# New instruction orders, a row of w4 in column halves, and roots on ScalarE in a two-layer spectral mixer kernel

## The chip, the cores and the metric

The kernel runs on one core of a Trainium2 chip. A core has TensorE (matrix products, called PE in the profile, its weight loads PEld), VectorE (DVE), ScalarE (ACT), GpSimd (POOL) and SyncE (SP), each with its own queue of instructions, worked off in order; an instruction waits at the head of its queue until what it reads has been written. DMA transfers are issued from the queues of SP, ScalarE and POOL. The metric is the device time of one execution in microseconds (us); the time before is the median of five runs.

## What is computed

Two layers, each a spectral filter followed by an MLP with token shifts, on x of 2048 tokens by 512 channels:

```python
def _A_ref(x, w_r, w_i):
    X = rfft2(x.astype(float32), axes=(-2, -1))
    X = X * (w_r + 1j * w_i)
    return irfft2(X, s=(S, D), axes=(-2, -1)).astype(bfloat16)

def _B_ref(x, w1, w2, w3, w4):
    h = _gelu(_layernorm(x, axis=-1) @ w1)
    c = D // 4
    g0 = jnp.pad(h[:, :, 0*c:1*c], ((0, 0), (1, 0), (0, 0)))[:, :S, :]
    g1 = jnp.pad(h[:, :, 1*c:2*c], ((0, 0), (0, 1), (0, 0)))[:, 1:, :]
    ...
    hs = jnp.concatenate([g0, g1, g2, g3], axis=-1) @ w2
    x1 = x + hs
    h2 = _gelu(_layernorm(x1, axis=-1) @ w3) @ w4
    return x1 + h2

x = A_x
x = x + _A_ref(_layernorm(x, axis=-1), A_w_r, A_w_i)
x = x + _B_ref(_layernorm(x, axis=-1), B_w1, B_w2, B_w3, B_w4)
x = x + _A_ref(_layernorm(x, axis=-1), A_w_r, A_w_i)
x = x + _B_ref(_layernorm(x, axis=-1), B_w1, B_w2, B_w3, B_w4)
```

A layernorm divides by the square root of the variance plus 1e-5, without gain or shift. Both layers use the same weights.

## The kernel before

Token 16 p + q lies in partition p and row q, so x is held as `K.x`, 128 partitions by 16 rows by 512 channels. All matrix products are bfloat16 with float32 sums in eight PSUM banks.

The order of all work is written out by hand in three strings. `ORDER_0` (L764) is the first front, `ORDER_A` (L769) is layer 0 with the front of layer 1 at its end, and `ORDER_B` (L788) is layer 1. A word is a letter for the operation and a number for the row, unit or group; the letter after the number is the engine (V for VectorE, A for ScalarE), the number after a dot the first PSUM bank. Words are emitted in that order, and every engine takes its own in that order. `manual_schedule` leaves it so. A word of `FLEX` (m, G, n, o, t, x, Y) can go to either engine.

The stages of a layer, with their letters:

- **Front.** Statistics of each row (s, or B in a later layer: bn_stats on VectorE, L266; rows 1 and 5 of the first front as sums on ScalarE), aggregation (i, or j; L295), the inverse deviation (S: a Sqrt on ScalarE and the reciprocal J on VectorE in the first front; two POOL operations with a power of -0.5, L302 and L303, in `rstd4`). The DFT table T is scaled by it (Q, 256 columns a row) and multiplied with x (O, four matmuls of 256 columns a row; `over_p`, or `over_p_plain` for five pairs of rows). The result is copied into V (G).
- **Spectral stage.** For ten units of one or two blocks (`UNITS`): over channels (d, 4 matmuls of 256 columns a block, L484), copy TV (t); over rows (q, on 64 partitions, L508), copy X (x); the product with the weights W (p, VectorE, L527); back over rows (b, 8 matmuls of 128 columns, L538), copy into hT (m). X has two buffers, TV and Y share four.
- **Back transforms.** Over channels (D, 8 matmuls of 256 columns for two rows, L556), copy Y; over tokens (P, 4 matmuls of 256 columns a row, L568); the residual add with a sum (a, VectorE, L576).
- **First norm.** A square with a sum on ScalarE (s, L279); for a group of four rows, the moments and the inverse deviation on POOL (r: `from_sums`, `rstd_twice`, `shift`; the power is L313) and a ratio used later (c, L315 to L323); the normalized rows (n); their transposition by DMA from SP's queue (T, `turn`, L592).
- **Mixer.** w1 (v, L607), gelu (h, L614), w2 with the token shifts (u, L623), residual (f, L631), second norm (k, R, o), its transposition (U).
- **MLP.** w3 (w, 8 matmuls of 512 columns, L658), gelu (g, L665), w4 (W, 14 matmuls of 512 columns a row, L671), residual (A, L676). Layer 1 stores each row (y). Layer 0 goes on with the front of layer 1. In layer 0 the words L and N reorder W and negate a part of the table TR.

`ROWS` (L760) gives the order of rows in the MLP and the next front: index 14 is row 0 and 15 is row 1. `fill` (L250) issues matmuls on zeros: `WAKE` (44) of them at the start, 2 or 3 behind some fronts of the first stage, and those of X words in the orders (X4.4 is four, into bank 4). At the end of `ORDER_A` there are 16.

Weights W come by 16 DMAs on SP's queue (`load_W`) behind the eight loads of x; row 32 of W, for both planes, by two DMAs on POOL's queue (L172). They are doubled across partitions by four DMAs on POOL's queue, W<-W (L183). The MLP weights follow on SP's queue behind a small gate transfer (L201).

Words z load the gelu table of ScalarE ahead of need (`gelu_table`, L728).

Of the kernel before, what the change touches and what calls it, by code (L numbers as in the profile page):

```python
# [153 lines left out]
def load_all(K, A_x, A_w_r, A_w_i, B_w1, B_w2, B_w3, B_w4):  # L154
# [16 lines left out]
    for pl, v in enumerate(planes):  # L171
        nc.gpsimd.dma_start(K.W[2::4, pl, 0], v[:, 32])  # L172
# [38 lines left out]
    nc.vector.memset(K.eps[:], EPS)  # L211
    K.mhalf = K.const.tile([P, 4], FP32, name="mhalf")
# [42 lines left out]
class Stats:  # L255
# [8 lines left out]
    def bn(self, i, src):  # L264
        st = self.K.small.tile([P, 6], FP32, name="ln_st")
        self.K.nc.vector.bn_stats(st[:], src)  # L266
        self.st[i] = st[:]
# [26 lines left out]
    def aggr(self, i):  # L294
        self.K.nc.vector.bn_aggr(self.mv[:, i, :], self.st.pop(i))  # L295
# [9 lines left out]
    def rstd_twice(self):  # L305

        K = self.K
        e = K.nc.gpsimd
        self.ve2 = ve2 = K.small.tile([P, 4], FP32, name="ln_ve2")
        self.r = K.small.tile([P, 4], FP32, name="ln_r")  # L310
        e.tensor_scalar(ve2[:], self.mv[:, :, 1], 0.0, 1.0 + EPS, op0=ALU.max, op1=ALU.mult)
        e.tensor_scalar(ve2[:], ve2[:], EPS * EPS, None, op0=ALU.add)
        e.tensor_tensor(self.r[:], ve2[:], K.mhalf[:], op=ALU.pow)  # L313

    def ratio(self):  # L315
        K = self.K
        e = K.nc.gpsimd
        ve = K.small.tile([P, 4], FP32, name="ln_ve")
        self.c = K.small.tile([P, 4], FP32, name="ln_c")
        e.tensor_scalar(ve[:], self.mv[:, :, 1], 0.0, EPS, op0=ALU.max, op1=ALU.add)  # L320
        e.tensor_tensor(ve[:], ve[:], K.mhalf[:], op=ALU.pow)
        e.tensor_tensor(self.ve2[:], self.ve2[:], self.r[:], op=ALU.mult)
        e.tensor_tensor(self.c[:], self.ve2[:], ve[:], op=ALU.mult)  # L323
# [88 lines left out]
def first_front(K):  # L412
# [47 lines left out]
    K.load_mlp()  # L460


def layer(K, last):
# [118 lines left out]
    def rstd2(g):  # L582
        ln[g].from_sums()
        ln[g].rstd_twice()
        ln[g].shift()
# [80 lines left out]

    def w4(n):
        g, i = divmod(n, 4)
        ps["W", n] = o = banks(K, 1)[:, 0]
        for t in range(14):  # L670
            nc.tensor.matmul(o, lhsT=gT[g][:, t, i * P:(i + 1) * P], rhs=K.w4[:, t, :],  # L671
                             start=(t == 0), stop=(t == 13))

    def add_x2(n):
        q = ROWS[n]
        nc.vector.tensor_tensor(K.x[:, q, :], ps.pop(("W", n)), K.x[:, q, :], op=ALU.add)  # L676
# [4 lines left out]
    def stats4(n):  # L681
        k, i = divmod(n, 4) if n < 12 else (n, 0)
        if k not in lnA:
            lnA[k] = Stats(K, n=4 if n < 12 else 1)
        lnA[k].bn(i, K.x[:, ROWS[n], :])
# [5 lines left out]
    def rstd4(k):  # L691
        lnA[k].rstd()
# [5 lines left out]
    def front(k):  # L698
        qs = [ROWS[n] for n in PAIRS[k]]
        ps["O", k] = over_p_plain(K, qs) if k < PLAIN else over_p(K, qs, k == 15)  # L700

    def take_front(k, eng):
# [9 lines left out]
        else:  # L712
            take_V(K, qs, ps["O", k], eng, k == 15)
# [14 lines left out]
    def gelu_table(_):  # L728

        t = K.small.tile([P, 1], FP32, name="wake")  # L730
        nc.scalar.activation(t[:], K.eps[:], ACT.Gelu_apprx_tanh, bias=0.0, scale=1.0)

    next_V = {}
    table = {"z": gelu_table, "d": over_d, "t": take_d, "q": over_q, "x": take_q, "p": weigh, "b": back_q,
# [22 lines left out]
UNITS = {b: [b, b + 1] if 2 <= b < 14 else [b] for b in (0, 1, 2, 4, 6, 8, 10, 12, 14, 15)}  # L757
LATE = ((14, 15), (0, 14))
# [6 lines left out]
s0 s2 i2 s3 i3 i0 s1 f0 s4 S0 J0 i4 Q1V Q0V s5 Q3V s6 s7 i6 i7 Q2A s11 s10 O0 G0A f1 S1 J1 s8 O1 G1A Q6A s9 Q7A i10  # L765
i11 Q4A i9 i8 S2 s12 Q5A J2 Q10A O3 s13 G3A Q11V i13 i12 Q9V Q8V s14 S3 s15 i14 i15 O2 J3 Q12V G2A S4 J4 O5 G5A Q15A
Q13V Q14V O4 G4V O6 G6A O7 G7V O8 G8V G8A
"""
ORDER_A = """  # L769
d0.5 t0A d1.7 t1V N0 d2.2 t2A q1.4 x1A q0.6 x0V p0 d4.0 p1 t4A d10.6 t10V d6.4 t6V q2.2 q4.6 x2A p2 x4A p4 d12.0 t12A  # L770
q10.3 q6.5 b0.7 x6A m0V b1.2 m1V p6 d8.0 x10A b5.5 b3.6 m5V t8A d15.7 m3A b2.2 p10 q8.0 m2A N1 t15V q12.4 x8A x12A
b4.2 p8 p12 d14.6 t14A b10.1 b11.3 m11A b6.7 m6V q14.5 x14A p14 q15.3 b9.0 m10A x15A p15 b7.6 m7A m9V b12.5 m12A m4A
b13.1 m13V b8.3 m8A b14.4 m14A b15.5 m15A m15V D1.2 D0.4 D3.6 Y0A Y3A Y1V P2.1 a2 P3.4 P0.3 P1.0 s2 a3 s3 a0 s0 a1 s1
D2.1 D4.4 Y4A P6.0 P7.3 Y2V a6 s6 a7 s7 P4.6 a4 P5.1 P9.4 D5.2 a5 r0 n0V s4 n1V s5 T0 r1 n3V P8.5 n2V Y5A D6.6 Y6A
D7.0 a9 Y7A a8 P11.4 a11 s11 n6V c0 n7V P10.3 n4V P15.1 s9 P12.0 s8 P14.2 n5V a10 a15 T1 a12 P13.5 a13 s10 r2 n9V n11V
n8V v0.6 v1.4 h0 c1 a14 T3 h1 T2 v3.0 s15 v2.6 s13 h3 u0.4 n10V T5 h2 u1.2 s12 f1 s14 u2.1 f2 k1 r3 c3 f0 E0 u3.7 n14V
T4 n15V f3 v5.2 n12A h5 v4.1 h4 u4.6 n13V k3 f4 L14 u5.5 u7.3 c2 k2 k0 E1 R0 f7 L13 E7 u6.7 T7 f5 T6 v6.1 E2 k4 h6 o1V
o2V o0A v7.3 E3 h7 u13.2 f6 o3A u11.6 f11 k11 k7 L12 u10.7 u15.1 f15 U0 f13 E13 f10 k10 u8.5 f8 u12.3 f12 u14.6 k5 U1
k6 w3.1 f14 E14 g3 z0 k13 L3 w1.5 g1 w4.0 g4 w0.3 g0 w2.1 g2 u9.5 f9 E6 k14 E9 E5 w6.3 E10 g6 w5.0 R1 g5 k8 E4 o4V o5V
L15 U2 W2.5 A2 W1.2 L7 o7V W0.3 A0 B2 k9 R2 j2 A1 o6A o10V U3 B0 w8.0 w7.4 L9 w12.6 g12 g8 W3.2 E8 g7 L2 B1 o9A w10.0  # L780
g10 w9.3 g9 E11 j0 L1 A3 o8A k12 B3 j3 o11A w11.0 g11 j1 S0 k15 w13.6 R3 g13 W5.2 W4.0 A5 U4 W6.3 U5 w17.6 A4 Q3 A6 B6
# [53 lines left out]
```

## Time and profile before

| what | us |
|---|---|
| median of five runs (349.51 to 351.24) | 350.13 |
| the profiled execution, its own time | 350.12 |
| its span, first to last instruction | 348.3 |
| first front, from the first real matmul to layer 0's first d | 8.25 to 19.28 |
| spectral stage of layer 0, to its first D | 19.28 to 39.40 |
| back transforms, norm, w1 of layer 0, to its first w2 | 39.40 to 61.34 |
| rest of layer 0, to the end of its last w4 row | 61.34 to 180.54 |
| layer boundary, to layer 1's first d | 180.54 to 185.45 |
| spectral stage of layer 1 | 185.45 to 205.30 |
| back transforms, norm, w1 of layer 1 | 205.30 to 226.93 |
| rest of layer 1, to its last residual add | 226.93 to 345.23 |

Matmuls overlap: one with 512 columns lasts 0.379 us in the profile, but the next starts 0.216 later. So the busy share of TensorE hides what it waits for, and the starts have to be compared. The granted TensorE clock is 0.999 over the span. The lines of the other tables are counted by instruction, with their mean duration: a square of a row 0.62 on ScalarE, a copy of 1024 columns 1.02 on ScalarE and 1.22 on VectorE, a statistic of a row 0.683 on VectorE.

### The profile page before, as it was taken

How to read it: one execution, taken by the hardware profiler on the slowest of the kernel's cores; microseconds unless marked ns; L12 is line 12 of the kernel's file. 1: busy time of each engine (PE TensorE's matmuls, PEld its weight loads, DVE VectorE, ACT ScalarE, POOL GpSimd, SP SyncE). 2: the span in 40 equal slices, each digit the busy share in tenths (PEclk: the TensorE clock that was granted, in tenths of full speed). 3: DMA queues.
4: the chain of work that ended last, by engine and by line, in shares of the span. 5: the costliest groups of instructions: out<-in, count | busy, mean ns of one | idle time of the engine just before them, and what ended most of it. 6: DMA issues, size and time to landing. Idle time of an engine off the chain costs nothing.

```text
span 348.3 us, 5561 instructions
## 1 busy us (share of the span) xinstructions
PE 338.8 (97%) x2120; PEld 188.5 (54%) x2120; DVE 185.8 (53%) x435; ACT 194.2 (56%) x337; POOL 73.5 (21%) x178
## 2 busy tenths in 40 slices
PE   8899999999999999999999999999999999999995
PEld 6668885444444444444558888544444444444442
DVE  5989796587439041285895979746514300302011
ACT  5969799766614714323417979984373373232230
POOL 4660056632020300002020005572004000100000
PEclk9999999999999999999999999999999999999999
DMA  7987935441020300210000001643002400300202
GB/s 236 308 307 249 374 91 101 82 69 19 7 55 1 60 2 0 55 37 1 0 2 0 2 2 29 122 94 62 1 2 49 102 0 2 75 0 2 90 15 90
DMA packets 44938, 24.35 MB, mean 70 GB/s; under 512 B 34768, under 2 KB 41904, under 8 KB 44912
## 3 DMA queue, kind: packets, MB, share of 16 engines
q1 hardware_dynamic: 43600, 19.97, 22.8%
q0 software_dynamic: 1168, 3.97, 3.4%
q8 instruction: 16, 0.26, 0.3%
q14 instruction: 10, 0.08, 0.1%
q10 hardware_dynamic: 144, 0.07, 0.1%
HBM read 11.41 MB, written 2.10 MB: 39 GB/s over the span
## 4 chain that ended last, share of the span: by engine, by line
PE 78%; DMA 9%; DVE 6%; ACT 3%; issue 1%; SPq 1%; DVEq 0%
PE ps L671 28%; PE ps L658 28%; PE ps L623 8%; PE ps L607 7%; DMA W<-in_A_w_i_dram 4%; PE ps L556 3%; DVE PB L527 2%; DMA xT<-xn 2%; DMA x_state<-in_A_x_dram 2%; PE ps L568 2%; DMA W<-W 1%; ACT hT L151 1%; ACT X L151 1%; DVE x_state L576 1%; DVE hT L149 1%
## 5 line engine op out<-in xcount | busy, mean ns | idle before, releaser
L665 ACT ACTIVATE gT<-ps 128x1024 bf16<-128x1024 f32 x56 | 56.0, 1022 | 87.3 <-PE ps L658 87.2
L658 PE MATMUL ps<-xT,w 128*128 128x512 bf16 x448 | 99.1, 379 | 0.0
L671 PE MATMUL ps<-w,gT 128*128 128x512 bf16 x448 | 99.1, 379 | 0.0
L676 DVE TENSOR_TENSOR x_state<-ps,x_state 128x512 bf16<-128x512 f32 x32 | 21.8, 688 | 99.2 <-PE ps L671 99.2
L658 PEld LDWEIGHTS <-w 128*128 128x128 bf16 x448 | 43.8, 98 | 52.6
L671 PEld LDWEIGHTS <-gT 128*128 128x128 bf16 x448 | 43.7, 98 | 52.4
L631 DVE SCALAR_TENSOR_TENSOR xn<-xn,ln_c,ps 128x512 bf16<-128x512 bf16 x32 | 23.2, 744 | 33.2 <-PE ps L623 26.0
L623 PE MATMUL ps<-w,hT 128*128 128x512 bf16 x128 | 29.1, 379 | 0.0
L607 PE MATMUL ps<-xT,w 128*128 128x512 bf16 x128 | 28.8, 379 | 0.3 <-DMA xT<-xn 0.3
L279 ACT ACTIVATE junk<-xn 128x512 bf16<-128x512 bf16 x32 | 19.9, 622 | 12.7 <-DVE xn L631 12.7
L285 POOL TENSOR_SCALAR ln_mv<-ln_s 128x4 f32<-128x4 f32 x16 | 4.6, 289 | 83.9 <-DVE x_state L576 49.6
L266 DVE BATCH_NORM_STATS2 ln_st<-x_state 128x6 f32<-128x512 bf16 x30 | 20.1, 683 | 3.4 <-DMA x_state<-in_A_x_dram 2.9
L576 DVE SCALAR_TENSOR_TENSOR x_state<-ps,x_state 128x512 bf16<-128x512 f32 x32 | 20.4, 685 | 1.9 <-PE ps L568 1.8
L614 ACT ACTIVATE hT<-ps 128x512 bf16<-128x512 f32 x32 | 18.0, 593 | 5.9 <-PE ps L607 5.5
L607 PEld LDWEIGHTS <-w 128*128 128x128 bf16 x128 | 12.3, 98 | 15.6 <-DMA xT<-xn 0.6
L623 PEld LDWEIGHTS <-hT 128*128 128x128 bf16 x128 | 12.5, 98 | 15.1 <-ACT hT L614 0.2
L279 ACT ACTIVATE xn<-x_state 128x512 bf16<-128x512 bf16 x32 | 19.8, 621 | 0.4
L527 DVE TENSOR_TENSOR PB<-X,W 128x2048 bf16<-128x2048 bf16 (+1 forms) x20 | 19.4, 1010 | 0.4 <-ACT X L151 0.2
L302 POOL TENSOR_SCALAR ln_ve<-ln_mv 128x4 f32<-128x4 f32 (+1 forms) x15 | 4.1, 274 | 70.4 <-DVE ln_mv L295 69.7
L484 PE MATMUL ps<-FA,V 128*128 128x256 bf16 x128 | 15.8, 273 | 0.7 <-ACT V L151 0.5
L538 PE MATMUL ps<-TR,PB 128*128 128x128 bf16 x256 | 16.3, 219 | 0.1
L568 PE MATMUL ps<-Y,Tinv 128*128 128x256 bf16 x128 | 15.6, 272 | 0.7 <-ACT Y L151 0.7
(83 smaller groups left out, 398.5 us busy)
## 6 DMA issues: line engine op xcount, KB each, us to landing
w<-in_B_w_dram SPq DMA_DIRECT2D x2, 1792.0 KB, 12.4
W<-W POOLq DMA_DIRECT2D x4, 514.0 KB, 5.0
x_state<-in_A_x_dram SPq DMA_DIRECT2D x8, 256.0 KB, 6.0
out_dram<-x_state SPq DMA_DIRECT2D x16, 128.0 KB, 1.9
TR<-tab_TR POOLq DMA_DIRECT2D x2, 512.0 KB, 6.5
w<-in_B_w_dram SPq DMA_DIRECT2D x2, 512.0 KB, 5.7
W<-in_A_w_r_dram SPq DMA_DIRECT2D x7, 128.5 KB, 7.8
W<-in_A_w_i_dram SPq DMA_DIRECT2D x7, 128.5 KB, 7.6
```

The source lines that it names most:

```text
L266: self.K.nc.vector.bn_stats(st[:], src)
L279: K.nc.scalar.activation(out, src, ACT.Square, bias=0.0, scale=D ** -0.5, accum_out=self.s[:, i, 1:2])
L527: nc.vector.tensor_tensor(t, X.pop(u)[:, 0:2 * n].unsqueeze(1).to_broadcast([P, 2, 2 * n, 256]), K.W[:, :, 2 * u:2 * u + 2 * n, 1:257], op ...
L568: nc.tensor.matmul(o[:, h * 256:(h + 1) * 256], lhsT=K.Tinv[:, c], rhs=rhs[:, ::-1] if h else rhs, start=(e == 0), stop=(e == 1))
L576: nc.vector.scalar_tensor_tensor(K.x[:, q, :], ps.pop(("P", q)), 1.0, K.x[:, q, :], op0=ALU.mult, op1=ALU.add, accum_out=ln[g].s[:, i, 0:1])
L607: nc.tensor.matmul(o[:, i], lhsT=K.w1[:, t, j * P:(j + 1) * P], rhs=xT[g][:, :, t, :], start=(t == 0), stop=(t == 3))
L623: nc.tensor.matmul(o, lhsT=K.hT[:, j, st:st + P], rhs=K.w2[:, j, :], start=(j == 0), stop=(j == 3))
L631: nc.vector.scalar_tensor_tensor(xn[:, q, :], xn[:, q, :], ln[q // 4].c[:, q % 4:q % 4 + 1], ps.pop(("u", n)), op0=ALU.mult, op1=ALU.add, ...
L658: nc.tensor.matmul(o[:, i], lhsT=K.w3[:, c, t * P:(t + 1) * P], rhs=xT3[g][:, :, c, :], start=(c == 0), stop=(c == 3))
L665: nc.scalar.activation(gT[g][:, 2 * j:2 * j + 2, :], ps.pop(("w", k)), ACT.Gelu_apprx_tanh, bias=0.0, scale=1.0)
L671: nc.tensor.matmul(o, lhsT=gT[g][:, t, i * P:(i + 1) * P], rhs=K.w4[:, t, :], start=(t == 0), stop=(t == 13))
L676: nc.vector.tensor_tensor(K.x[:, q, :], ps.pop(("W", n)), K.x[:, q, :], op=ALU.add)
```

## The change

Six things change.

1. The two DMAs that load row 32 of W are issued from ScalarE's queue.
2. Behind the loads of the MLP weights, SP's queue gets one transposing DMA of the tile of zeros into a spare tile of the xT buffers.
3. In layer 0 the row with index 14 goes through w4 in two halves of 256 columns (words W14 and W24, A14 and A24, B14 and B24); its statistics are two partial ones, aggregated together.
4. For groups 0 and 1 of the first norm of each layer the deviation is a Sqrt on ScalarE (e) and a reciprocal on VectorE (i), in place of a power on POOL; the ratio takes the deviation.
5. For the rows with indices 12 to 15 in the front of layer 1 the same is done with `std` and `invert` (S and J).
6. The front of index 14 is split over two banks and copied by both engines, as that of index 15 was, and all three orders are new, with new engines for some copies and other numbers of dummy matmuls (7 at the end of `ORDER_A`, 4 ahead of its first d).

```diff
-        nc.gpsimd.dma_start(K.W[2::4, pl, 0], v[:, 32])
+        nc.scalar.dma_start(K.W[2::4, pl, 0], v[:, 32])
...
+    K.eps2 = K.const.tile([P, 1], FP32, name="eps2")
+    nc.gpsimd.memset(K.eps2[:], EPS * EPS)
...
-    def bn(self, i, src):
-        st = self.K.small.tile([P, 6], FP32, name="ln_st")
-        self.K.nc.vector.bn_stats(st[:], src)
-        self.st[i] = st[:]
+    def bn(self, i, src, part=(0, 1)):
+        k, n = part
+        if i not in self.st:
+            self.st[i] = self.K.small.tile([P, n, 6], FP32, name="ln_st", padded_shape=[P, 2, 6])[:]
+        self.K.nc.vector.bn_stats(self.st[i][:, int(k)], src)
...
+    def rstd_twice(self, root=False):
...
+        self.root = root
         e.tensor_scalar(ve2[:], self.mv[:, :, 1], 0.0, 1.0 + EPS, op0=ALU.max, op1=ALU.mult)
+        if root:
+            return
         e.tensor_scalar(ve2[:], ve2[:], EPS * EPS, None, op0=ALU.add)
         e.tensor_tensor(self.r[:], ve2[:], K.mhalf[:], op=ALU.pow)
+
+    def std_twice(self):
+        K = self.K
+        self.sd = K.small.tile([P, 4], FP32, name="ln_sd", bufs=4)
+        K.nc.scalar.activation(self.sd[:], self.ve2[:], ACT.Sqrt, bias=K.eps2[:], scale=1.0)
+
+    def invert_twice(self):
+        self.K.nc.vector.reciprocal(self.r[:], self.sd[:])
+        self.shift()
...
         e.tensor_tensor(ve[:], ve[:], K.mhalf[:], op=ALU.pow)
+        if self.root:
+            e.tensor_tensor(self.c[:], self.sd[:], ve[:], op=ALU.mult)
+            return
...
+    spare = K.grp.tile([P, 4, 4, P], BF16, name="xT", bufs=4)
+    K.nc.sync.dma_start_transpose(spare[:, 0, 0:1], K.zeros[:])
...
-        ln[g].rstd_twice()
-        ln[g].shift()
+        ln[g].rstd_twice(g in ROOT)
+        if g not in ROOT:
+            ln[g].shift()
...
+    def columns(n):
+
+        if last or n % 10 != 4 or n < 14:
+            return n, slice(0, D)
+        return 14, slice(0, D // 2) if n == 14 else slice(D // 2, D)
...
-        ps["W", n] = o = banks(K, 1)[:, 0]
+        r, d = columns(n)
+        g, i = divmod(r, 4)
+        ps["W", n] = o = banks(K, 1)[:, 0, 0:d.stop - d.start]
         for t in range(14):
-            nc.tensor.matmul(o, lhsT=gT[g][:, t, i * P:(i + 1) * P], rhs=K.w4[:, t, :],
+            nc.tensor.matmul(o, lhsT=gT[g][:, t, i * P:(i + 1) * P], rhs=K.w4[:, t, d],
                              start=(t == 0), stop=(t == 13))
...
     def rstd4(k):
-        lnA[k].rstd()
+        if k < 12:
+            lnA[k].rstd()
+        else:
+            lnA[k].std()
+
+    def invert4(k):
+        lnA[k].invert()
...
-        ps["O", k] = over_p_plain(K, qs) if k < PLAIN else over_p(K, qs, k == 15)
+        ps["O", k] = over_p_plain(K, qs) if k < PLAIN else over_p(K, qs, k >= 14)
...
+ROOT = (0, 1)
```

`add_x2` and `stats4` take the same columns, and `take_front` splits its copy for k >= 14. `gelu_table` becomes `act_table`, whose word z0 still loads the gelu table. Of the orders, the parts that the prediction walks through:

```diff
-s0 s2 i2 s3 i3 i0 s1 f0 s4 S0 J0 i4 Q1V Q0V s5 Q3V s6 s7 i6 i7 Q2A s11 s10 O0 G0A f1 S1 J1 s8 O1 G1A Q6A s9 Q7A i10
-i11 Q4A i9 i8 S2 s12 Q5A J2 Q10A O3 s13 G3A Q11V i13 i12 Q9V Q8V s14 S3 s15 i14 i15 O2 J3 Q12V G2A S4 J4 O5 G5A Q15A
-Q13V Q14V O4 G4V O6 G6A O7 G7V O8 G8V G8A
+s0 s2 s3 i0 i2 i3 s1 f0 S0 s4 J0 Q2V Q3V O1 i4 s5 s7 s6 Q1A Q0A i7 i6 G1A f1 S1 O0 G0A s11 s10 i11 J1 Q6A i10 s8 s9
+Q7A Q4A i8 i9 s13 Q5A s12 S2 J2 i13 i12 Q10V O3 G3A Q11A O2 Q8V O5 Q9A s15 s14 S3 J3 i15 i14 G2A S4 Q13V Q12V J4 Q14V
+G5A Q15A O4 O6 G6A G4V O7 G7V O8 G8A G8V
...
-O2.0 G2A O1.3 G2V L11 G1A G1V W15.6 Q8 A15 B15 j15 S15 Q12 W13.7 A13 Q9 Q11 Q10 B13 j13 W14.1 O5.4 G5A O4.2 Q15 A14
-B14 O15.6 G15A S13 G4A j14 S14 Q13 O6.0 G15V G6A X4.4 Q14 O14.5 G14A X8.6 X4.5 G4V
+W12.7 L7 j11 j9 O3.5 W15.4 j8 A12 B12 G3A G3V A15 B15 S2 Q10 z0 j15 S15 Q8 J15 j12 W13.2 Q15 W24.5 Q9 W14.3 A13 B13
+j13 S13 S12 Q11 A24 J13 Q13 O4.0 G4A J12 B24 Q12 A14 B14 j14 S14 O15.6 G15V G15A J14 Q14 O5.4 G5A O6.2 G4V O14.6 G14V
+G6A G14A X4.5 X3.4 L6
...
-v0.6 v1.4 h0 c1 a14 T3 h1 T2 v3.0 s15 v2.6 s13 h3 u0.4
+v0.6 r2 v1.3 s15 c2 h0 a13 h1 T2 a12 n9V T3 v3.5 s12 n8V T4 h3 n11V v2.3 u0.0
```

In the new orders the copies whose engine changes are these. Spectral stage of layer 0: TV of units 0, 4 and 14 to VectorE, of 1 and 10 to ScalarE; back-copies of 5, 6 and 13 to ScalarE, of 8 to VectorE. Layer 1: all TV copies on ScalarE; X of units 4 and 10 on VectorE, of 1 and 14 on ScalarE; back-copies of 1, 12, 0, 14 and 3 to ScalarE, of 13, 9, 7 and 2 to VectorE. Back transforms of layer 0: only Y2 stays on VectorE; of layer 1: Y0 and Y4, where Y0, Y3 and Y7 were.

## The prediction

> **What bounds the kernel now.** First the engines' totals on the page, then the same by stretch, then TensorE's own waits, then the instructions in order of time around the layer boundary.
>
> ```profile
> PE 338.8 (97%) x2120; PEld 188.5 (54%) x2120; DVE 185.8 (53%) x435; ACT 194.2 (56%) x337; POOL 73.5 (21%) x178
> ...
> core 0: us, PE busy (x) PEld busy (x) DVE busy (x) ACT busy (x) POOL busy (x), PEclk, DMA share, GB/s
> 19.28:39.40 20.12, 19.47 (x257) 16.08 (x257) 18.55 (x25) 17.89 (x25) 4.87 (x6) 1.00 0.84 291
> 185.45:205.30 19.85, 19.10 (x259) 16.22 (x256) 16.72 (x21) 17.91 (x26) 0.00 (x0) 1.00 0.01 2
> 39.40:61.34 21.94, 21.26 (x160) 15.42 (x161) 16.28 (x46) 19.58 (x43) 10.86 (x31) 1.00 0.57 148
> 205.30:226.93 21.63, 21.28 (x161) 15.55 (x162) 16.67 (x45) 19.52 (x47) 10.23 (x31) 1.00 0.34 64
> 58.00:180.00 122.00, 122.00 (x590) 56.26 (x589) 67.88 (x170) 56.14 (x95) 23.06 (x52) 1.00 0.15 29
> ```
>
> TensorE is busy for 97%, but the stretches differ. From 58 to 180 us (the mixer and MLP of layer 0), and after 227 us, it never waits: 512-column matmuls start every 0.216 us, 256-column ones every 0.108, 128-column ones every 0.055 (differences of starts in the timeline). That work is not changed in amount, so nothing is to be won there, and only a new order that stalls can lose. In the two spectral stretches (first two rows) three engines are nearly full at once: VectorE 18.55 and ScalarE 17.89 of 20.12, then 16.72 and 17.91 of 19.85. In the next two (back transforms and first norm) ScalarE is at 19.58 of 21.94. A microsecond moved from one engine's queue to another's counts there.
>
> ```profile
> PE ps L371 <- DMA W<-in_A_w_i_dram: 1.2, 1, 1.2
> ...
> PE ps L568 <- ACT Y L151: 0.7, 2, 0.5
> PE ps L371 <- DVE ln_r L343: 0.5, 1, 0.5
> PE ps L484 <- ACT V L151: 0.5, 1, 0.5
> PE ps L556 <- ACT hT L151: 0.5, 1, 0.5
> PE ps L556 <- DVE hT L149: 0.5, 1, 0.5
> PE ps L607 <- DMA xT<-xn: 0.3, 2, 0.2
> ```
>
> These are TensorE's waits: small, and all at the seams between stages. (The first names a DMA; at 12.00 us ScalarE had just written the scaled table that matmul reads, so I read it as ScalarE's.) Measured from start to start each is some 0.15 longer, as a matmul's end is drawn late. The largest waste hides as work: dummy matmuls at the layer boundary.
>
> ```profile
> 180.74 0.69 DVE L676 TENSOR_TENSOR x_state<-ps,x_state 128x512 bf16<-128x512 f32 x1 [0.55 <-PE ps L671]
> ...
> 181.47 0.69 DVE L266 BATCH_NORM_STATS2 ln_st<-x_state 128x6 f32<-128x512 bf16 x1
> ...
> 182.77 0.56 POOL L303 TENSOR_TENSOR ln_r<-ln_ve,mhalf 128x1 f32<-128x1 f32 x1
> ...
> 184.14 1.47 PE L252 MATMUL ps<-zeros 128*128 128x256 bf16 x12
> 185.45 2.78 PE L484 MATMUL ps<-FA,V 128*128 128x256 bf16 x24
> ```
>
> The last w4 row leaves TensorE at 180.54. Its residual add, statistics and inverse root run one after another to 183.66, and layer 1 begins at 185.45: 4.91 us. Of these 16 dummy matmuls are 16 x 0.108 = 1.73 and a gap 0.1; the real fronts are 3.07.
>
> **The change part by part.** *W row 32.* Two issues leave POOL's queue (0.78 and 0.55 us at 1.27) and go behind the T load on ScalarE's (0.36 at 0.73). At 0.5 to 0.8 each they end near 2.4; the table load (1.28) and the first Sqrt (0.20) then end near 3.9, when x lands (3.89). Nothing; the landing of x covers it, and without that cover up to 0.3. POOL's first real operation is at 4.70, and the first W copy waits until 12.60 for a later load. *Dummy transposition.* One issue on SP behind the w4 load (issues end at 32.21) and ahead of the first real one at 49.44: 17 us of cover for its 1.23, landing some 3.2 later. The shown issues take 1.23 to 1.35 and land in 3.0 to 3.7, so it can win 0.5 at most, and I take nothing. The spare tile takes one of four xT buffers, wanted back only for the fourth group.
>
> *First front* (8.25 to 19.28). Scaled tables on VectorE go from 9 to 7, on ScalarE from 7 to 9. At 0.23 each VectorE gains 0.46; at 0.45 each ScalarE loses 0.9, of which one falls in its idle 0.90 ahead of 9.33. I followed both queues: the last copies into V end 0.3 later if ScalarE sets the end, 0.45 sooner if VectorE does. I take +0.2; kept: -0.45 to +0.6.
>
> *Spectral, layer 0.* ScalarE: two more back-copies (2 x 0.48), one small TV less (0.6): +0.4. VectorE: -2 x 0.62 + 0.65 = -0.6. The fuller engine goes from VectorE's 18.55 to ScalarE's 18.3. I take -0.25; kept: +0.4 (ScalarE's load added whole) to -0.9 (its idle between copies closed as well). *Spectral, layer 1.* ScalarE: two small TV (+1.0), two big X given and two small taken (-0.84), one back-copy (+0.48): +0.64. VectorE: -1.3 + 1.0 - 0.6 = -0.9. Here ScalarE was the fuller, but its idle of 1.2 between copies (0.27, 0.30, 0.18, 0.20, 0.30 in the timeline) shrinks to some 0.4 when I follow the new queue. I take +0.2; kept: -0.5 to +0.65.
>
> *Back transforms and norms.* Groups 0 and 1 lose two POOL operations (0.23, 1.04) and gain a ScalarE root (0.29, from the 128x4 roots of the start) and a reciprocal (0.16): 0.8 shorter each. The first Y copy starts after one D unit (8 x 0.108 = 0.87) and not after two or three. Layer 0 now: 128 matmuls x 0.108 = 13.8 of work in 39.40 to 54.11 (14.7), then a 0.32 wait. ScalarE pays: the copy of Y1 moves to it (+0.95), two roots (+0.6), one more square ahead of the first gelu (+0.6). I take -0.7; kept: -1.0 (all seams closed) to +0.4 (ScalarE's 2.15 less its 0.87 earlier start and the 0.9 of seams). *Layer 1*: the same, with group 1's transposition some 0.4 earlier, but Sqrt is now ScalarE's table when the layer starts, so a Gelu load comes ahead of its first gelu, which layer 1 did not have:
>
> ```profile
> 54.76 1.28 ACT L614 ACT_TABLE_LOAD   x1
> 56.06 2.30 ACT L614 ACTIVATE hT<-ps 128x512 bf16<-128x512 f32 x4
> ```
>
> In layer 0 the load costs 1.28, the gelu following in 0.02. Queued behind it are the gelus, whom w2's matmuls await. ScalarE: 1.28 + 0.6 + 0.95 (one more Y) - 2 x 0.61 (squares put later) = +1.6, less 0.9 from the earlier start: gelus 0.7 late. I find w2's second row waiting 0.4 for one. Seams -0.6, this +0.4: I take -0.2; kept: -0.9 to +0.9.
> The Trainium skill ("ScalarE: Activation LUTs", section "What ACT_TABLE_LOAD costs") speaks against this change: each switch of set costs the 1283 ns load plus about 1380 ns of drain. The row beside it shows the load and no drain; by the page the whole forecast would come out 1.4 us later, 350.3 (an estimate from that page).
>
> *Layer boundary.* After the row's second half leaves TensorE: hand-off 0.2, half an add 0.42 (the 128x256 adds of L395), half the statistics (no row; 0.34 as half of 0.683, whole 0.68 at worst), aggregate 0.18, hops 0.2, root 0.29, reciprocal 0.15, scale 0.26: 2.04, against 3.12 now. The fronts ahead take 2.63 anyway, so the row's own front no longer waits. ScalarE's last copies (group of O6 1.02 from 2.85, then 0.38) end at 4.25, layer 1 starts at 4.4 instead of 4.91; only 7 dummies are left (0.76). Two halves of w4 are 28 x 0.108 = 3.02, as 14 x 0.216 was. The Sqrt load falls where ScalarE idles (9.35 us before 181.66); without that cover 1.28. I take -0.5; kept: -0.9 to +0.2. *Four new dummies* ahead of d0 (0.43) lie in the wait of 0.68 at 19.28. *The end*: the last w4 row, its add (0.69) and store stay last; nothing.
>
> Sum: +0.2 - 0.25 + 0.2 - 0.7 - 0.2 - 0.5 = **-1.25**. The profiled execution took 350.12 (span 348.3 and 1.8 around it), the median of the runs is 350.13. Forecast 348.9, own range 347.2 to 349.9.
>
> **Rivals.** *Given back*: what boundary and roots win (1.4) is eaten by the copies moved to ScalarE; spectral stages at +0.4 and +0.65, first front +0.3: 350.12 - 1.4 + 1.35 = 350.1. For it: ScalarE at 89 to 90% in four stretches; against: VectorE was fuller in the first spectral one. *ScalarE becomes the bound*, slower: its queue in layer 1's norm stretch cannot take the 1.6. Place: the gelus before w2; price 0.9 there, 1.35 in the three stages above, nothing won in layer 0's norm stretch, less 0.5 of the boundary: +1.75, 351.9. It decides as soon as ScalarE's added 1.6 exceeds the 0.9 of earlier start by more than the 0.6 of seams. Against: the whole must miss at once. *Nothing from the roots*: VectorE is in its adds when the reciprocal is ready, and the norms start no sooner; then -1.25 + 0.8 = -0.45, 349.7, within the next class.
>
> **How the numbers follow.** Forecast 0.47 (under 349.1 nearly all), given back or roots worthless 0.26, slower 0.27. About 0.3% (1.05 us) is what a measurement here tells from no change: faster 0.47, within 0.26, slower 0.27. Adding the kept ends of the six terms gives -4.65 to +3.15, which will not all fall together: the range is 346.9 to 351.9.
>
> **What will show it.** Right: layer 1's first matmul under 4.6 us after the last w4 half, groups 0 and 1 normalized sooner after their last square, no wait at the first w1 row, spectral stretches of at most 20.0. Wrong: ScalarE without a gap there while TensorE waits for it, a wait on gelu before w2 beyond 0.5, or any TensorE wait inside the MLP.

## The result and the profile after

| | before | changed |
|---|---|---|
| median, us | 350.38 (56 runs) | 349.79 (31 runs, 348.49 to 350.63) |
| ratio of the times, 95% interval | 1 | 0.9981 (0.9973 to 0.9989) |
| profiled execution, us (its span) | 350.12 (348.3) | 350.23 (348.4) |

The change saves 0.19%, some 0.6 us (the medians differ by 0.59, the ratio gives 0.67), where 1.25 were forecast. The profiled execution of the changed kernel lies 0.4 above the median of its runs and 0.1 above that of before, so its own waits must be read with care. First its totals, then the six stretches that were shown of before (columns: stretch and its length, then PE, PEld, DVE, ACT and POOL busy with the number of instructions, clock, DMA share, GB/s):

```profile
PE 339.1 (97%) x2129; PEld 189.0 (54%) x2129; DVE 185.4 (53%) x444; ACT 197.2 (57%) x350; POOL 62.9 (18%) x157
```

```profile
19.47:39.96 20.49, 19.57 (x256) 15.96 (x257) 18.80 (x24) 18.18 (x26) 5.43 (x6) 1.00 0.80 276
39.96:61.46 21.50, 21.33 (x161) 15.59 (x161) 15.42 (x47) 20.37 (x46) 9.65 (x29) 1.00 0.67 179
61.46:181.12 119.66, 119.53 (x591) 56.28 (x590) 66.53 (x171) 54.84 (x91) 17.27 (x39) 1.00 0.14 27
181.12:185.36 4.24, 4.00 (x42) 3.39 (x39) 4.06 (x14) 3.38 (x6) 0.00 (x0) 1.00 0.00 0
185.36:205.03 19.67, 19.01 (x257) 16.31 (x258) 16.53 (x20) 18.23 (x29) 0.00 (x0) 1.00 0.01 2
205.03:226.63 21.60, 21.27 (x160) 15.53 (x161) 15.88 (x46) 20.32 (x46) 6.45 (x22) 1.00 0.26 50
```

The spectral stage of layer 0 (first row) became longer, 20.49 against 20.12. The back transforms and norm of layer 0 became shorter (21.50 against 21.94), the boundary too (4.24 against 4.91), the spectral stage of layer 1 a little (19.67 against 19.85). The norm of layer 1 stands still. VectorE did not fall in the first row, although its queue was given less to do: 18.80 against 18.55. That is the first thing to be explained.

The waits of TensorE in the changed kernel (us in total, times, longest):

```profile
PE ps L389 <- ACT Tq L378: 1.2, 1, 1.2
...
PE ps L576 <- ACT hT L151: 0.4, 1, 0.4
PE ps L576 <- DVE hT L149: 0.4, 1, 0.4
...
PE ps L528 <- DVE TV L149: 0.4, 1, 0.4
PE ps L588 <- DVE Y L149: 0.3, 1, 0.3
```

The wait for a transposition ahead of w1 (L607 of before, now L628) is gone. New is a wait for a TV copy of VectorE (L528, in layer 0's spectral stage, at 25.79). The differences of starts show one more, which this list leaves out: 0.28 before the first w3 matmul at 82.61, in a stretch where before had none.

The boundary of the layers, as the timeline has it:

```profile
180.80 0.49 PE L699 MATMUL ps<-w,gT 128*128 128x256 bf16 x3
...
181.33 0.42 DVE L705 TENSOR_TENSOR x_state<-ps,x_state 128x256 bf16<-128x256 f32 x1
...
181.78 0.43 DVE L270 BATCH_NORM_STATS2 ln_st<-x_state 128x6 f32<-128x256 bf16 x1
...
182.49 0.29 ACT L358 ACTIVATE ln_r<-ln_mv,eps 128x1 f32<-128x1 f32 x1
...
182.82 0.16 DVE L361 RECIPROCAL ln_r<-ln_r 128x1 f32<-128x1 f32 x1
...
183.02 0.29 DVE L376 TENSOR_SCALAR Tq<-T,ln_r 128x256 bf16<-128x256 bf16 x1
...
184.19 0.93 PE L254 MATMUL ps<-zeros 128*128 128x256 bf16 x7
185.36 0.83 PE L504 MATMUL ps<-FA,V 128*128 128x256 bf16 x6 [0.24 <-ACT V L151]
```

From the end of w4 to the scaled table it is 183.31 - 181.12 = 2.19 us, where 2.04 were forecast and 3.12 stood before. Layer 1 begins 4.24 after w4, with ScalarE's last copy into V.

### The profile page after: what moved, and what is told of

The parts are those of the page before. It is cut to its first block, busy times and chain, and to the rows that moved or that the text cites. A ratio compares the mean times of both kernels' runs of the same rounds, so it can differ in the third digit from the quotient of the medians.

```text
span 348.4 us, 5581 instructions
## 1 busy us (share of the span) xinstructions
PE 339.1 (97%) x2129; PEld 189.0 (54%) x2129; DVE 185.4 (53%) x444; ACT 197.2 (57%) x350; POOL 62.9 (18%) x157
## 5 line engine op out<-in xcount | busy, mean ns | idle before, releaser
L699 PE MATMUL ps<-w,gT 128*128 128x512 bf16 (+1 forms) x462 | 99.3, 373 | 0.0
L705 DVE TENSOR_TENSOR x_state<-ps,x_state 128x512 bf16<-128x512 f32 (+1 forms) x33 | 22.0, 674 | 97.7 <-PE ps L699 97.7
L699 PEld LDWEIGHTS <-gT 128*128 128x128 bf16 x462 | 45.1, 98 | 51.3
L628 PE MATMUL ps<-xT,w 128*128 128x512 bf16 x128 | 28.7, 379 | 0.0
L270 DVE BATCH_NORM_STATS2 ln_st<-x_state 128x6 f32<-128x512 bf16 (+1 forms) x31 | 20.1, 665 | 4.3 <-DMA x_state<-in_A_x_dram 3.9
L628 PEld LDWEIGHTS <-w 128*128 128x128 bf16 x128 | 12.3, 98 | 15.0 <-issue 0.7
L151 ACT ACTIVATE TV<-ps 128x1024 bf16<-128x1024 f32 (+1 forms) x15 | 14.4, 981 | 3.6 <-PE ps L504 2.3
L305 POOL TENSOR_SCALAR ln_ve<-ln_mv 128x4 f32<-128x4 f32 x11 | 3.3, 303 | 71.8 <-DVE ln_mv L298 71.1
L576 PE MATMUL ps<-G,hT 128*128 128x256 bf16 x128 | 15.3, 273 | 0.8 <-ACT hT L151 0.4
```

The source lines that it names most:

```text
L270: self.K.nc.vector.bn_stats(self.st[i][:, int(k)], src)
L576: nc.tensor.matmul(o[:, i, e * 256:(e + 1) * 256], lhsT=M[:, F, e, 2 * m + i, :], rhs=K.G[:, F, e, :], start=(F == 0 and e == 0), stop=(F ...
L628: nc.tensor.matmul(o[:, i], lhsT=K.w1[:, t, j * P:(j + 1) * P], rhs=xT[g][:, :, t, :], start=(t == 0), stop=(t == 3))
L705: nc.vector.tensor_tensor(x, ps.pop(("W", n)), x, op=ALU.add)
```

## The experiments

All times are medians in us, all ratios are to the kernel before, with 95% intervals; the changed kernel has 0.9981 (0.9973 to 0.9989). The kernel before was run again beside each group of experiments, with medians of 350.17 to 350.63, so two kernels of different groups are compared by their ratios. "Stage" is the spectral stage of layer 0, from TensorE's first d to its first D.

### The parts of the change, one at a time

**e1: old orders of the first front and the first spectral stage.**

```diff
 ORDER_0: as before
-N0 X4.6 d0.5 t0V d1.7 t1A d2.2 t2A q0.0 x0V p0 ... m15V m15A
+d0.5 t0A d1.7 t1V N0 d2.2 t2A q1.4 x1A q0.6 x0V p0 ... m15A m15V
```

> The changed kernel with the first front and the spectral stage of layer 0 in the order of before; all else as changed. Theory (ScalarE took more copies than its queue holds): the first front ends 0.2 us sooner, the spectral stage takes 20.1 us instead of 20.49, and the whole kernel 0.4 to 0.6 us less than the changed one. Rival (the stages after it set the pace, so an earlier start is waited away): the first w2 matmul stays at 61.4 to 61.5 us and the whole time does not move.

Measured: 351.61, ratio 1.0032 (1.002 to 1.0043). Front and stage were sooner, as the theory had it (first D at 39.35 instead of 39.96, stage 20.13), and the time still rose by 1.8. (That the order itself made the stage sooner did not hold up, see the last group.) In its trace TensorE waits 1.01 at 54.90 and 1.02 at 238.57, places that this edit does not touch:

```profile
PE ps L628 <- DMA xT<-xn: 1.7, 2, 0.9
```

The transpositions that it waits for (view of the tile xT between 49.9 and 51.4 us):

```profile
L616 SPq DMA_TRANSPOSE xT<-xn x2: 1262/1759/2256, 49.1 to 50.5; - x2
...
DMA to landing us min/median/max: 4.3/4.3/4.4
```

One issue took 2256 ns instead of 1.23 to 1.35 us, and both landed after 4.3 to 4.4 us instead of 3.0 to 3.3. At 50.41 the trace's DMA records have a piece of 16 KB on the queue q8, kind "instruction". A new theory: a fetch of instructions that starts while a transposition is in flight holds it up, and where the fetches fall depends on how many instructions TensorE has had before.

**e2: no roots in the norms.**

```diff
-ROOT = (0, 1)
+ROOT = ()
 the words e0, e1, i0, i1 of both layers removed
```

> The changed kernel with the power on POOL for groups 0 and 1 again (no Sqrt on ScalarE, no reciprocal on VectorE there). Theory (the reciprocal stands behind residual adds in VectorE's queue, so little was won): each back-transform-and-norm stage changes by 0.3 us at most, either way. Rival (the prediction's: 0.8 us shorter chains set the stages): the two stages grow by 0.7 to 1.0 us together.

Measured: 351.40, ratio 1.0022 (1.0012 to 1.0032); the theory of a small worth fell. The two norm stretches of this kernel:

```profile
39.52:61.92 22.40, 21.66 (x161) 15.49 (x161) 15.21 (x45) 19.98 (x43) 12.47 (x35) 1.00 0.61 159
205.98:228.10 22.12, 21.57 (x161) 15.55 (x161) 15.70 (x44) 20.23 (x44) 9.02 (x26) 1.00 0.25 49
```

22.40 against 21.50 and 22.12 against 21.60: in the new order, which was written for them, the roots are worth 0.9 and 0.5 us, though the new order without them is slower than the old one (21.94 and 21.63). Some of the 0.9 is a transposition, issued at 50.62, that landed in 3.6.

**e3: the last w4 row of layer 0 whole.**

```diff
-        if last or n % 10 != 4 or n < 14:
+        if True:
...
-... W24.5 ... A24 ... B24 ...
```

> The changed kernel with the last w4 row of layer 0 whole again (one bank, one add, one statistic), the rest of the boundary as changed. Theory (the fronts of the other rows, 2.63 us, cover the chain either way): the boundary stays under 4.4 us, the whole time within 0.2. Rival (the halves brought the 0.67 us): the boundary goes back to 4.8 to 4.9.

Measured: 352.20, ratio 1.0041 (1.0026 to 1.0057). The boundary took 4.73 instead of 4.24, so the halves are worth 0.49. The rest of the loss is again a transposition: issued at 234.10, landed after 5.1, with pieces of 16 and 8 KB 2.5 and 3.3 us behind its issue; TensorE waited 1.81 at 239.22.

**e4: without the dummy transposition, and with row 32 on POOL's queue.**

```diff
-        nc.scalar.dma_start(K.W[2::4, pl, 0], v[:, 32])
+        nc.gpsimd.dma_start(K.W[2::4, pl, 0], v[:, 32])
...
-    spare = K.grp.tile([P, 4, 4, P], BF16, name="xT", bufs=4)
-    K.nc.sync.dma_start_transpose(spare[:, 0, 0:1], K.zeros[:])
```

> The changed kernel without the early transposing DMA and with row 32 of W loaded from POOL's queue again. Theory: both are covered, the first w1 matmul stays within 0.2 us of 54.50 and the whole time within 0.3. Rival (the first transposition of a run pays something once, and the early one pays it out of sight): the first real transpositions land later and the first w1 matmul comes 0.5 us or more later.

Measured: 349.84, ratio 0.9982 (0.997 to 0.9994), that of the changed kernel: no worth of the two parts can be told in the whole time.

### Do hidden dummies move the time?

**f1 and f3: e1 and e3 again, with dummy matmuls in waits that are there anyway.**

```diff
 as e1_old_fronts, and
-FILL = {0: 3, 1: 3, 2: 2, 3: 2, 4: 2}
+FILL = {0: 3, 1: 14, 2: 2, 3: 2, 4: 2}
 and X4.6 (4 dummies) ahead of the first d
```

> The kernel with the old first front and spectral order (which took 351.61) with 15 more dummy matmuls in two waits of the first 20 us; nothing else differs. Theory (TensorE's instructions come in 16 KB pieces by DMA; a transposing DMA in flight when such a piece is fetched lands 1 to 2 us late): 30 more instructions ahead bring each later fetch forward, by 1.6 us at 50 us and by 3.2 at 234 us, away from the transpositions at 49.1, 50.5, 232.9 and 234.3; these land in 3.1 to 3.4 us, TensorE's two waits of 1.0 us there vanish, and the whole time falls to 349.0 to 349.7. Rival (the old order itself does not fit the norm stage of the changed kernel): the waits stay and the time stays at 351.3 to 351.9.

```diff
 as e3_whole_row, and
-FILL = {0: 3, 1: 3, 2: 2, 3: 2, 4: 2}
+FILL = {0: 15, 1: 3, 2: 2, 3: 2, 4: 2}
 and X6.6 for X4.6
```

> The kernel with the whole last w4 row (which took 352.20) with 14 more dummy matmuls in waits of the first 20 us, so that TensorE has as many instructions as in the changed kernel. Theory: the wait of 1.8 us at the second pair of w1 groups of layer 1 vanishes; what stays is the boundary's 4.7 us against 4.24, so 350.2 to 350.5. Rival (the whole row itself costs it): 351.9 to 352.5.

Measured: 350.28, ratio 0.9999 (0.9983 to 1.0014), and 350.79, ratio 1.0013 (1.0004 to 1.0022). By the ratios, fifteen and fourteen more matmuls on zeros made the kernels 1.2 and 1.0 us faster than without them; the waits of 1.0 and 1.8 were gone. Both fell short of what was expected (349.0 to 349.7 and 350.2 to 350.5). In the traces the stage took 20.63 in f1 and 21.01 in f3, and the w3 waits were 0.38 and 0.30.

**f2: the changed kernel without the dummies of the front.**

```diff
-FILL = {0: 3, 1: 3, 2: 2, 3: 2, 4: 2}
+FILL = {}
-N0 X4.6 d0.5 ...
+N0 d0.5 ...
```

> The changed kernel without the 16 dummy matmuls of the first front (12 between its fronts, 4 ahead of the first d), which all stand where TensorE waits anyway. Theory (fetches against transpositions): TensorE's fetches come later by 1.7 us at 50 us and 3.5 us at 232 us, into the transpositions at 49.8/51.1 and 232.5/233.8; TensorE waits 0.5 to 2 us at the first or third pair of w1 groups and the whole time rises to 350.5 to 352. Rival (dummies are only waste): the time stays at 349.8 or falls by up to 0.2.

Measured: 350.72, ratio 1.001 (0.9996 to 1.0024). With less to do the kernel was slower by 1.0. In the trace a transposition issued at 50.13 landed after 5.0, with a piece of 16 KB 2.67 behind it, and TensorE waited 1.19 at 56.06. But that trace has a second cause, in the front itself. Without the dummies TensorE had no matmul from 9.62 to 12.12 us, and its granted clock (the third figure from the end of this row of the stretch 12 to 14 us) was 0.50:

```profile
12.00:14.00 2.00, 1.88 (x10) 1.33 (x10) 2.00 (x6) 1.45 (x5) 0.00 (x0) 0.50 1.02 319
```

The first front took 12.19 instead of 11.36. Three of the twelve runs have a mean clock of 0.993 or 0.994, the others 0.998 to 1.000. So f2 does not measure the fetches alone; how its 1.0 us divides is not shown.

**g2: the kernel before with 8 more dummies.**

```diff
-FILL = {0: 3, 1: 3, 2: 2, 3: 2, 4: 2}
+FILL = {0: 3, 1: 11, 2: 2, 3: 2, 4: 2}
```

> The kernel before with 8 more dummy matmuls in a wait of TensorE that is there anyway (10.65 to 12.0 us), nothing else. Theory (the 16 KB instruction fetches of TensorE and the transposing DMAs that are in flight when one starts hold each other up): the fetch that stood at 235.24 us comes about 1.7 us sooner, into the flight of the transpositions issued at 230.16 and 231.50, and the one at 49.19 comes at about 48.3; TensorE waits 0.5 to 1.5 us more in one of these places, the time is 350.8 to 351.8 us although no work was added to any path. Rival: hidden dummies cost nothing, 350.2 to 350.5 us.

Measured: 350.40, ratio 1.001 (0.9999 to 1.002): the theory's price did not come. The fetch did fall where it was wanted, and the transpositions of 230.29 and 231.63 landed late, after 4.5 and 4.1, but TensorE reached them later still and did not wait. A late landing costs only where the row is due.

In the traces of the sixteen kernels of this case there are 512 transpositions of rows, by what fetch started between 0.2 us ahead of their issue and 2.85 behind it:

```
fetch            transpositions   landing min/median/max us   3.6 us or more
none                  409            3.0 / 3.1 / 3.3               0
8 KB                   72            3.0 / 3.3 / 4.2              15
16 KB                  31            3.0 / 4.1 / 5.1              22
```

### The wait at the first w3 matmul

**f4 and g1: the copies of the first rows drawn forward.** In f4 on top of f1, in g1 alone.

```diff
-... o3A f7 v6.0 u8.3 f8 o2V h6 u11.4 o1A E4 u9.0 u15.5 E0 o0V ...
+... o3A f7 o2V E0 v6.0 u8.3 f8 h6 u11.4 o1A o0V E4 u9.0 u15.5 ...
```

> The padded kernel with the old first front and spectral order, and three words of layer 0's second norm moved forward on VectorE (normalized rows 2 and 0 of the MLP order ahead of a w2 residual), so that the transpositions for the first w3 are issued 1 to 2 us sooner. Theory: the wait of 0.3 to 0.6 us at the first w3 (82.6 us in the changed kernel) vanishes and the whole time is 0.3 to 0.5 below that of the padded kernel. Rival (that wait is paid somewhere else anyway): no difference between the two.

> The changed kernel with the two copies of layer 0's first rows (row blocks 0's transposition inputs of the third MLP product) drawn forward in the written order, nothing else. Theory: the wait of 0.28 us before the first matmul of w3 at 82.6 us of the changed kernel is a transposition issued at 77.71 that landed in 3.9 us; issued a few us sooner it lands before TensorE wants it. The wait goes, the w1-to-w4 stretch of layer 0 falls from 119.66 to about 119.4, the time to 349.3 to 349.5 us. Rival: the wait is not on the path (the same time is lost at the next matmuls), the time stays at 349.6 to 349.9.

Measured: 349.63, ratio 0.9983 (0.9973 to 0.9993), and 349.59, ratio 0.9987 (0.9971 to 1.0002). In both traces the w3 wait is gone, and the rest of layer 0 takes 119.42 and 119.41 instead of 119.66. In the changed kernel the transposition of 77.71 landed after 3.9, an 8 KB piece having started 2.58 behind it, and the next one, of 79.03, landed at 82.48, 0.13 ahead of that matmul; before, the last of this pair landed at 79.81 for a first w3 at 81.20. The saving of 0.25 is smaller than what these runs can tell of the whole time: f4 lies 0.65 under f1, but 0.51 of that is the stage in its trace (20.12 for 20.63).

### The spectral stage of layer 0

**g3: two copies given back to VectorE.**

```diff
-m5A ... m13A
+m5V ... m13V
```

> The changed kernel with the two back copies of the spectral stage of layer 0 that the change gave to ScalarE returned to VectorE. Theory (ScalarE's load set the length of the stage): from the first matmul of the stage to its end 20.1 to 20.2 us instead of 20.49, the time 0.2 to 0.4 us below the changed kernel, 349.4 to 349.6. Rival (the new order itself, not the engine of the copies): the stage stays at 20.4 to 20.6 and the time at 349.7 to 350.0; a fetch that moves is no part of either, since no instruction of TensorE changes.

Measured: 350.54, ratio 1.0014 (1.0002 to 1.0027); both theories fell. The stage took 21.97, and now VectorE was full, 20.48 us in a stretch of 22.00:

```profile
19.40:41.40 22.00, 19.72 (x259) 15.95 (x258) 20.48 (x26) 17.73 (x24) 4.90 (x6) 1.00 0.77 277
```

Less load on ScalarE did not shorten the stage. VectorE's instructions one by one show what made it longer. First those of the changed kernel: the first two products with W on VectorE and the TV copies behind them, and POOL's operations on the second half of the table TL (the words are start, duration, engine, line, operation):

```profile
22.68 1.85 DVE L547 TENSOR_TENSOR PB<-X,W 128x1024 bf16<-128x1024 bf16 x2
24.45 2.47 DVE L149 CAST TV<-ps 128x1024 bf16<-128x1024 f32 x2
```

```profile
21.19 1.67 POOL L230 TENSOR_SCALAR TL<-TL 128x512 bf16<-128x512 bf16 x1
22.76 1.26 POOL L231 COPY TL<-TL 128x512 bf16<-128x512 bf16 x1
```

Then those of g2, the kernel before with 8 more dummies:

```profile
21.80 2.31 DVE L527 TENSOR_TENSOR PB<-X,W 128x1024 bf16<-128x1024 bf16 x2
```

```profile
21.25 1.68 POOL L228 TENSOR_SCALAR TL<-TL 128x512 bf16<-128x512 bf16 x1
22.82 0.78 POOL L229 COPY TL<-TL 128x512 bf16<-128x512 bf16 x1
```

And those of the kernel before:

```profile
22.64 1.30 DVE L527 TENSOR_TENSOR PB<-X,W 128x1024 bf16<-128x1024 bf16 x2
```

There the two products took 1.30 together (694 and 685 ns), and POOL had finished at 22.17. In the changed kernel and in g2 the second takes 1168 and 1692 ns. In g2 POOL's copy ends at 23.60 and the product 0.5 after it, as if it had stood still until POOL was done. TensorE pays for it through the TV copies, which stand behind the products in VectorE's queue: its wait for them at 25.79 is 0.52 from start to start in the changed kernel, 1.25 at the same place in g3, and h3 (below), where the products are not lengthened, has none there.

The Trainium skill ("SBUF — State Buffer", section "SBUF: two separate sides") says that GpSimd and certain VectorE operations take a port pair in turns, as a lock held for a whole instruction. The second products agree with it: in the changed kernel, g2 and g3 they end 0.5 after POOL's copy. The first ones agree only in part: in g2 the first product ran from 21.80 in its usual 694 ns, all of it inside POOL's operation of 21.25 to 22.93. POOL's spans in a profile are rough; what the two engines share no run here shows.

POOL does this work behind a W copy that waits for a load (in the changed kernel 2.10 us, by its timeline), so it slides with the landing of that load. By trace, with what the products and the negated table (word N0, 0.42 alone) took too long, in us:

```
kernel                 POOL's pair     products   N0      stage
old order, N0 behind the first TV
  h2 (below)           18.93-21.24       0.07     0.00    20.14
  f4                   19.32-21.95       0.05     0.13    20.12
  before               19.55-22.17       0.07     0.03    20.12
  e1                   19.68-22.30       0.05     0.21    20.13
  f1                   20.78-23.63       0.51     0.00    20.63
  g2                   21.25-23.60       1.02     0.00    21.09
new order, N0 first
  e4                   18.80-21.38       0.05     1.44    20.87
  f2                   19.61-22.17       0.03     1.14    20.42
  e3                   20.01-22.49       0.02     0.37    20.07
  g1                   20.63-23.47       0.53     0.01    20.48
  e2                   20.75-23.60       0.80     0.00    20.73
  changed              21.19-24.03       0.52     0.00    20.49
```

(Left out are f3, where a product also waited 0.84 for a W copy, stage 21.01, and g3, whose products lost 1.26 of its 21.97.) In the old order the stage is 20.05 to 20.12 plus what the products lose, in all six. The new order has put N0 ahead of the first TV copy, at 19.57 instead of 21.11: there it also meets POOL when POOL is early. Of what N0 loses only a part reaches TensorE: it waits 0.77 at 21.45 in e4, where N0 lost 1.44.

**h1, h2 and h3: POOL's pair out of the way.** In h1:

```diff
         double(0)
         turn_TL(K, slice(0, 8))
-        double(1)
         turn_TL(K, slice(8, 16))
+        double(1)
...
-N0 X4.6 d0.5 t0V
+X4.6 d0.5 t0V N0
```

> The changed kernel with POOL's second pair of table operations (128x512, some 1.67 and 0.77 us) ahead of the second W copy that waited for a load, and VectorE's negated table (word N0) behind the first TV copy, as it stood before. Theory (overlap with POOL stretches VectorE's products: 739 and 1168 ns in the changed kernel's trace where 694 and 685 stood before): POOL has finished by 21 us, the first two products take 0.69 each, the spectral stage of layer 0 takes 19.9 to 20.1 us, the time is 349.2 to 349.5 us. Rival (the new order is slower in itself): the stage stays at 20.4 or above, the time at 349.7 to 350.0.

In h2 the same move of POOL's pair, without that of N0, in the kernel before:

> The kernel before with the same move of POOL's second table pair and nothing else. Theory: in its profiled execution the two did not meet, so the stage stays at 20.05 to 20.15 us; in executions where a load lands later they would have met, so the median may fall a little, 349.9 to 350.4 us. Rival (the move itself shortens or lengthens something): a stage under 19.9 or over 20.3, or a time outside these.

In h3, h1 with the copies drawn forward as in g1:

> The changed kernel with the move of h1_tables_apart and the drawn-forward copies of g1_early_rows. Theory: both found waits (0.5 in the spectral stage, 0.28 at the first w3 matmul) are gone and add up: stage of 19.9 to 20.1, first w3 without a wait, 349.0 to 349.3 us, some 1 us under the kernel before. Rival (executions differ in where the loads and instruction fetches fall, so one trace's waits say little of the median): 349.5 to 349.9.

Measured:

| kernel | median | ratio | stage | first w3 waits |
|---|---|---|---|---|
| h1_tables_apart | 349.44 | 0.9962 (0.995 to 0.9975) | 20.03 | 0.70 |
| h2_before_tables_apart | 350.38 | 0.9993 (0.9982 to 1.0004) | 20.14 | none |
| h3_apart_and_early | 348.91 | 0.9946 (0.9931 to 0.9961) | 20.05 | none |

The stage falls to 20.03 and 20.05 in the new order, with ScalarE nearly as busy as in the changed kernel (18.08 in h3, 18.18 there), and stays in the old, as the theory had it. In h1 the w3 wait grew to 0.70, with a transposition of 77.74 that landed after 3.9, 1.92 ahead of a fetch; h3 has neither wait. Its trace, VectorE and POOL at the place shown above, and the stage:

```profile
21.96 1.36 DVE L547 TENSOR_TENSOR PB<-X,W 128x1024 bf16<-128x1024 bf16 x2
```

```profile
17.59 1.64 POOL L230 TENSOR_SCALAR TL<-TL 128x512 bf16<-128x512 bf16 x1
19.14 0.77 POOL L231 COPY TL<-TL 128x512 bf16<-128x512 bf16 x1
```

```profile
18.75:38.80 20.05, 19.49 (x256) 15.87 (x256) 18.27 (x24) 18.08 (x26) 3.78 (x6) 1.00 0.86 295
```

h3, at 348.91 a little under its 349.0 to 349.3, is faster than both kernels: its interval lies below that of the changed kernel (0.9973 to 0.9989), by 1.2 us from ratio to ratio. Against h2, the kernel before with the same move of POOL's pair, it is some 1.6 us faster (0.9946 to 0.9993).

## Why the direction was right and the size was not

The time fell by 0.6 us where 1.25 were forecast. By the prediction's terms, from the traces (rest of layer 0 and boundary are taken together, since fronts can move across the end of w4):

| stretch | before | changed | h3 | changed less before | h3 less before | forecast |
|---|---|---|---|---|---|---|
| first front | 11.03 | 11.37 | 10.82 | +0.34 | -0.21 | +0.2 |
| spectral, layer 0 | 20.12 | 20.49 | 20.05 | +0.37 | -0.07 | -0.25 |
| norms, layer 0, to the first w2 | 21.94 | 21.50 | 21.45 | -0.44 | -0.49 | -0.7 |
| rest of layer 0 and boundary | 124.11 | 123.90 | 123.66 | -0.21 | -0.45 | -0.5 |
| spectral, layer 1 | 19.85 | 19.67 | 19.67 | -0.18 | -0.18 | +0.2 |
| norms, layer 1, to the first w2 | 21.63 | 21.60 | 21.61 | -0.03 | -0.02 | -0.2 |

- **Boundary: right.** The chain came out at 2.19 for 2.04 forecast, layer 1 starts 4.24 after w4 for 4.4, and without halves the boundary takes 4.73. Half the statistics took 0.43, nearer to half (0.34) than to the whole (0.68). The Sqrt load fell into ScalarE's idle time (at 172.98), as said.
- **Spectral stage of layer 0: the step that failed.** I took -0.25, from the fuller engine (18.55 to 18.3); it came out at +0.37. With POOL's pair out of the way (h3) it is -0.07, smaller than forecast though no worse than before. The rest, 0.44 from stage to stage, came from products that took 0.52 longer beside POOL, and from TensorE's wait for the copy behind them. I had counted VectorE's durations as fixed and taken POOL's 4.87 us in that stretch for work of no account. The prediction's own range, +0.4 to -0.9, held the value by luck: its upper end was ScalarE's added load, and that was not what did it (g3, h3).
- **Mixer and MLP of layer 0, where "only a new order that stalls can lose": the sentence was right, its term of nothing was not.** The new order stalls at the first w3, 0.28 here and 0.3 to 0.7 in nine other kernels with it, none with the rows drawn forward. I had named a wait inside the MLP as a sign of error, and put no price on it.
- **Norms, layer 0: mis-sized**, -0.44 for -0.7. The roots do shorten the chain, but their reciprocal queued behind two adds on VectorE:

```profile
47.41 0.29 ACT L324 ACTIVATE ln_sd<-ln_ve,eps 128x4 f32<-128x4 f32 x1
```

```profile
47.50 0.68 DVE L596 SCALAR_TENSOR_TENSOR x_state<-ps,x_state 128x512 bf16<-128x512 f32 x1
...
48.11 0.69 DVE L596 SCALAR_TENSOR_TENSOR x_state<-ps,x_state 128x512 bf16<-128x512 f32 x1
...
48.72 0.17 DVE L327 RECIPROCAL ln_r<-ln_sd 128x4 f32<-128x4 f32 x1
49.00 0.41 DVE L366 TENSOR_SCALAR xn<-x_state,ln_mv,ln_r 128x512 bf16<-128x512 bf16 x1
```

  The root is done at 47.70, the reciprocal starts at 48.72, the first normalized row at 49.00 (before: 48.68). The rival "nothing from the roots" described this and gave 349.7, close to what was measured, but by luck: without roots the new order is 0.9 and 0.5 slower. What it won came at the later rows, and no wait is left at the first w1.
- **Norms, layer 1**: -0.03 for -0.2. The table load was there, the gelus behind it with no drain, as in the row of before, so the 1.4 us that the prediction estimated from the Trainium skill ("ScalarE: Activation LUTs", section "What ACT_TABLE_LOAD costs") did not come:

```profile
222.11 1.28 ACT L635 ACT_TABLE_LOAD   x1
223.40 1.08 ACT L635 ACTIVATE hT<-ps 128x512 bf16<-128x512 f32 x2
```

- **Spectral stage of layer 1**: -0.18 for +0.2. ScalarE's busy time rose by 0.32 (17.91 to 18.23) where 0.64 were counted, and its idle time fell by 0.50 (1.94 to 1.44). The prediction's own figures, +0.64 of work less 0.8 of idle time, come to -0.16, not to the +0.2 that was taken. No POOL work stands in that stretch.
- **First front**: +0.34 in one trace, -0.21 in another with the same order: it moves with the landing of x and W, and this case has no run that sets its worth.
- **Row 32 and the dummy transposition: nothing**, and e4 shows nothing against it.
- **The end: forecast as nothing**, but the rest of layer 1 to the end of the program takes 121.81 instead of 121.42, in h3 as well. Of this, 0.27 lies behind the landing of the last store (1.61 to the end of the span instead of 1.34; e2, without the roots, has 1.15); no run shows why.
- **"Given back" and "ScalarE becomes the bound"** were both wrong in mechanism: ScalarE rose to 20.37 and 20.32 in the norm stretches and no stretch got longer by it.

With the end, and with what comes ahead of the first real matmul (8.25 before, 8.10 in the changed kernel, 7.93 in h3), the terms add up to +0.1 for the changed kernel and -1.35 for h3, as their profiled executions do (350.23 and 348.76 against 350.12). So the one trace of the changed kernel does not show its median's gain of 0.6 at all. Its first front alone is 0.55 longer than that of h3, which has the same front order, and such differences come with the loads. One trace a kernel places a wait, but it cannot share out 0.6 us to the tenth.

The medians carry the answer: without the two collisions the new order is some 1.6 us faster than the old one (h3 against h2), and with them 0.6. The forecast's 1.25 is nearer to what the edits are worth without the collisions, though that is partly chance: single terms were off by up to 0.4. What failed is that the new order's neighbours were not costed, POOL beside VectorE and a transposition due sooner than it lands.

What stays open: how often POOL's pair meets VectorE over many executions (one profile a kernel shows one), how a fetch holds up a transposition, and why the two collisions are worth 1.2 us in the medians and 0.72 in the traces.

## What to carry to other kernels

Durations from a profile hold for the neighbours that an instruction had there: ask for each moved VectorE operation that reads and writes SBUF what POOL does in the same microsecond. Before you believe a difference of 1 us between two versions of a long kernel, look whether a transposing DMA landed late beside an instruction fetch, and draw such transpositions forward until their landing is not due. To cost one part of a change, take it out and compare stretches; whole times mix the part with where the fetches fall.

## What was not expected of the hardware

- Instructions come by DMA while the kernel runs, in pieces of 16 KB on one queue and of 8 KB on another; those of 16 KB move with the count of TensorE's instructions (at 50.41 in e1, at 48.18 in f1 with 15 matmuls more ahead). A transposition in flight with a 16 KB piece landed after 3.6 to 5.1 us in 22 of 31 cases, with a piece of neither size never after more than 3.3 (409 cases). Fifteen and fourteen matmuls on zeros made two kernels 1.2 and 1.0 us faster (f1, f3).
- In f2 TensorE had no matmul from 9.62 to 12.12 us, and its granted clock was 0.50 for 3.4 us from 11.72. No other trace of this case has less than the full clock before its last matmul; e1, with 1.6 us without a matmul (10.20 to 11.81), kept it.
- VectorE's negation of a 128x1024 bfloat16 table took 1.86 us beside POOL instead of 0.42 (e4):

```profile
18.90 1.86 DVE L760 TENSOR_SCALAR TR<-TR 128x1024 bf16<-128x1024 bf16 x1
```

- The dummy transposition, issued at 33.76 behind large loads, took 10.65 us to issue and landed after 16.1, where later ones take 1.23 and 3.1; nothing waited for it.
